# A six-layer cross network on one core: turning the first group on TensorE, and reordering the last two groups

## The chip, the cores and the metric

The kernel runs on one core of one Trainium2 chip. The metric is the device time of one execution in microseconds (us). A profiled execution also gives its span, from the first to the last instruction. In the profiled execution of the kernel before, the time is 1.8 us more than the span (491.88 against 490.1). Positions inside an execution are counted from the start of the span.

Names: TensorE is PE in the profile, VectorE is DVE, ScalarE is ACT, GpSimd is POOL, SyncE is SP. "SPq" and "ACTq" lines are DMA issues by SyncE and ScalarE. PE "products" are matmuls of a layer; "turning" is a transposition on PE by a product with the identity. A "filler" is a product whose result nobody reads; it only keeps PE busy. The "granted clock" is the share of its full clock that PE was given according to the profile's records: 1.00 is full, 0.50 is half.

## The reference

```python
# x0: [16384, 416], ws: [6, 416, 416], bs: [6, 416], all bf16
x = x0
for l in range(6):
    proj = einsum('bd,de->be', x, ws[l]) + bs[l]
    x = x0 * proj + x
return x
```

## The kernel before

The 16384 rows are 8 groups of 2048 rows, each of 4 chunks of 512. The 416 features are three tiles of 128 and a tail of 32. A job (g, l) is layer l of group g; 48 jobs run in an order that interleaves the groups. Rows are kept transposed (features on the partitions), so a job is three tiles of 12 full products (128 x 128 weights, 512 columns), 4 products for the tail rows of the weights (`rows32`), and, batched over some jobs (`tails`), the 32 output features of the tail. ScalarE adds the bias and takes the result out of PSUM, VectorE multiplies with x0 and adds x.

The head: of group 0, chunks 0 and 1 are loaded as they lie in memory ("natural") and turned on PE; chunks 2 and 3 come by DMA transposes.

```python
    add("act", lambda h: h.dma_start(bs_sb[0:L, :], bs[:, :]), ...)
    load_nat(0, 0, 2)          # chunk 0, its first half: 208 KB
    load_nat(0, 2, KK)         # and its second
    load_wm(0, "sp")           # the weights of layer 0: 312 KB
    load_nat(1, 0, KK)         # chunk 1: 416 KB
    load_w3(0, "sp")
    make_wbd(0)
    half = slice(2 * CH, GC)
    ...                        # transpose of the tail
    for t in range(NT):
        add("sp", lambda h, t=t: h.dma_start_transpose(
            x0s[0][:, t * GC + 2 * CH:(t + 1) * GC], g0[half, t * P:(t + 1) * P]), ...)
    ...
def first_job():
    transposed_chunk(0)        # 12 + 4 turns on PE, 2 ScalarE and 2 VectorE copies out of PSUM
    ...                        # bias turned
    full(g, l, 0, ba, True, True, chunks=[0])
    transposed_chunk(1)
    ...
    full(g, l, 0, ba, True, True, chunks=[1])
    full(g, l, 1, bb, True, True, chunks=[0, 1])
    full(g, l, 0, ba, True, True, chunks=[2, 3])
    rows32(g, l, 0, ba, False)
    ...
```

The end: group 6 leaves by DMA transposes out of the transposed form (4 small ones for the tail, 3 large ones, "main turns"), then one store of 1664 KB. Layer 5 of group 7 is computed with the rows on the partitions: its input is turned on PE (`to_rows`) and four row sets kk (every fourth row) are computed and stored one by one. (The first line of the cut stands below `output` in the kernel.)

```python
    where[((LAST, L - 2), 0)] = batches[-1]     # the last tails: behind tile 0 of job (7, 4)
    ...
    def output(g):
        ...
        for j in range(NJ):
            add("sp", lambda h, ...: h.dma_start_transpose(ost[...], x3s[s3][q, :]), ...)  # tail
        if g == LAST - 1:
            turn(0)
            turn(1)
        turn(2)
        ...                                      # the store, 1664 KB
    ...
    to_rows(0, bka)
    layer_rows(0, bkb)
    to_rows(1, bka)
    layer_rows(1, bkb)
    layer_rows(2, bka)
    layer_rows(3, bkb)
```

The job order ends (6,4), (7,4), (6,5), and then (7,5) in the row form.

Of the kernel before, what the change touches and what calls it, by code (L numbers as in the profile page):

```python
# [198 lines left out]
def bass_standalone__cross_network_dcn__recsys_kernel(  # L199
# [57 lines left out]
    def x0_tok(s, t, j):  # L257
        return ("x0", s, t, j)
# [21 lines left out]
    def load_wm(l, eng):  # L280
        add(eng, lambda h: h.dma_start(wm[l][:, :, :], ws[l, 0:NT * P, :].rearrange("(t p) f -> p t f", p=P)),
            writes=[("wm", l)], lane=f"wm{l}", batch=0)
# [189 lines left out]
    def load_nat(j, k0, k1):  # L472
        add("sp", lambda h: h.dma_start(x0n[:, j, k0:k1, :], perm(g0, j)[:, k0:k1, :]),  # L473
            writes=[("nat", j, k) for k in range(k0, k1)], lane=f"nat{j}{k0}", batch=0)

    add("dve", lambda h: h.memset(warm[:, :], 0.0), writes=["warm"])
    add("act", lambda h: h.activation(warm[:, :], warm[:, :], ACT_F.Identity, bias=0.0, scale=1.0),
        reads=["warm"], writes=["warm"])
    add("act", lambda h: h.dma_start(bs_sb[0:L, :], bs[:, :]), writes=["bs_sb"], lane="bs", batch=0)
    load_nat(0, 0, 2)  # L480
    load_nat(0, 2, KK)
    load_wm(0, "sp")
    load_nat(1, 0, KK)
    load_w3(0, "sp")
    make_wbd(0)
    half = slice(2 * CH, GC)
    add("sp", lambda h: h.dma_start_transpose(tw[NTW - 1][:, half], g0[half, D - P:D]),  # L487
        writes=[("tw", NTW - 1, j) for j in (2, 3)], lane="Tb0", batch=0)
    for t in range(NT):
        add("sp", lambda h, t=t: h.dma_start_transpose(  # L490
            x0s[0][:, t * GC + 2 * CH:(t + 1) * GC], g0[half, t * P:(t + 1) * P]),
            writes=[x0_tok(0, t, j) for j in (2, 3)], lane=f"x0_00{t}", batch=0)
    load_wm(1, "sp")
    load_w3(1, "sp")
    load_group(1)
# [2 lines left out]
    make_wbd(1)  # L498
    make_wbd(2)

    for _ in range(14):
        add("pe", lambda h: h.matmul(psum[:, 7 * CH:7 * CH + P], ident[:, :], ident[:, :], start=True, stop=True),
            reads=["ident"], writes=[("ps", 7)])

    def psum_t(b):
        return psum[:, b * CH:(b + 1) * CH].bitcast(BF16)
# [30 lines left out]
    def first_job():  # L537

        g, l = 0, 0
        start_job(g, l)  # L540
        transposed_chunk(0)
        bt = 7
        for t in range(NT):
            add("pe", lambda h, t=t: h.transpose(
                psum_t(bt)[:, t * 8:t * 8 + L], bs_sb[0:L, t * P:(t + 1) * P], ident[0:L, 0:L]),
                reads=["bs_sb", "ident"], writes=[("ps", bt)])
        for j in range(NJ):
            q = slice(j * T32, (j + 1) * T32)
            add("pe", lambda h, j=j, q=q: h.matmul(
                psum_t(bt)[q, NT * 8:NT * 8 + L], bs_sb[0:L, NT * P:D], ident[0:L, 0:L],  # L550
                is_transpose=True, tile_position=(0, j * T32)),
                reads=["bs_sb", "ident"], writes=[("ps", bt)])
        add("act", lambda h: h.activation(
            bias[:, :, :], psum_t(bt)[:, 0:32].rearrange("p (t l) -> p t l", l=8)[:, :, 0:L], ACT_F.Copy),
            reads=[("ps", bt)], writes=["bias"])
        ba, bb = [4, 5, 6, 7], [0, 1, 2, 3]
        full(g, l, 0, ba, True, True, chunks=[0])
        transposed_chunk(1)
        for j in (2, 3):
            q = slice(j * T32, (j + 1) * T32)  # L560
            add("act", lambda h, q=q, j=j: h.dma_start(
                x0s[0][q, XW:XW + CH], tw[NTW - 1][P - T32:P, j * CH:(j + 1) * CH]),
                reads=[("tw", NTW - 1, j)], writes=[("x03q", 0, j)], lane="x03_00", batch=0)
        full(g, l, 0, ba, True, True, chunks=[1])
        full(g, l, 1, bb, True, True, chunks=[0, 1])
        full(g, l, 0, ba, True, True, chunks=[2, 3])
        rows32(g, l, 0, ba, False)
        evacuate(g, l, 0, ba, [0, 1], 2, vector=[2, 3])
        full(g, l, 1, bb, True, True, chunks=[2, 3])
        rows32(g, l, 1, bb, False)  # L570
        rows32(g, l, 2, ba, True)
        evacuate(g, l, 1, bb, list(range(NJ)), 2)
        full(g, l, 2, ba, False, True, lambda j: evacuate(g, l, 2, ba, [j], 1))
        finish_tile(g, l, NT)
        tails([(g, l)])
# [19 lines left out]
    def output(g):  # L595

        s, s3 = xset[(g, L)], xtail[(g, L)]
        def turn(t):
            add("sp", lambda h: h.dma_start_transpose(
                ost[:, :, t * P:(t + 1) * P], xs[s][:, t * GC:(t + 1) * GC]),  # L600
                reads=[("x", s, t, j) for j in range(NJ)], writes=[("ost", t)], lane="ot", batch=g)

        if g < LAST - 1:
# [3 lines that stand above are left out]
            q = slice(j * T32, (j + 1) * T32)  # L607
            add("sp", lambda h, j=j, q=q: h.dma_start_transpose(
                ost[:, j * KK:(j + 1) * KK, NT * P:D], x3s[s3][q, :]),
                reads=[("x3", s3)], writes=[("ost", NT, j)], lane="ot", batch=g)  # L610
# [4 lines that stand above are left out]
        rows = out[g * GC:(g + 1) * GC, :]  # L615
        o = ost[:, :, :].rearrange("p (j k) f -> p j k f", j=NJ)
        parts = [("(j k p) f -> p j k f", 0, NJ)]
        if g == 0:
            parts = [("(j p k) f -> p j k f", 0, 2), ("(j k p) f -> p j k f", 2, NJ)]
        for pat, j0, j1 in parts:  # L620
            add("sp", lambda h, pat=pat, j0=j0, j1=j1: h.dma_start(
                rows[j0 * CH:j1 * CH, :].rearrange(pat, j=j1 - j0, k=KK), o[:, j0:j1, :, :]),
                reads=[("ost", t) for t in range(NT)] + [("ost", NT, j) for j in range(NJ)],
                writes=[("out", g, j0)], lane="out", batch=g)
        free_x.append(s)
        free_3.append(s3)

    items = []
    where = {(b[min(1, len(b) - 1)], 0): b for b in batches[:-1]}
    where[((LAST, L - 2), 0)] = batches[-1]  # L630
    del where[((0, 0), 0)]
    for jb in order[1:-1]:
        for i in range(NT):
            items.append(("tile", jb, i))
            if (jb, i) in where:
                items.append(("tails", where[(jb, i)]))


    single = 0
# [84 lines left out]

    first_use = {"x5": True, "on": True}

    def to_rows(kp, bks):

        for j in range(NJ):
            for h2 in range(2):  # L730
                for t in range(NT):
                    o = h2 * CH + t * P
                    add("pe", lambda h, j=j, t=t, kk=2 * kp + h2, o=o: h.transpose(  # L733
                        psum_t(bks[j])[:, o:o + P], xcol(t, j, kk), ident[:, :]),
                        reads=[stok(t, j), "ident"], writes=[("ps", bks[j])])
        for h2 in range(2):
            for j in range(NJ):
                q = slice(j * T32, (j + 1) * T32)
                o = h2 * CH + NT * P
                add("pe", lambda h, j=j, q=q, kk=2 * kp + h2, o=o: h.matmul(  # L740
                    psum_t(bks[j])[:, o:o + T32], x3col(j, kk), ident[q, q], is_transpose=True,
                    tile_position=(j * T32, 0)),
                    reads=tok3 + ["ident"], writes=[("ps", bks[j])])
        for j in range(NJ):
            extra = x0_all(s5) + x03_toks(s5) if first_use.pop("x5", None) else []
            eng = "act" if j % 2 == 0 else "dve"
# [46 lines left out]
        add("dve", lambda h: h.tensor_tensor(o, o, x5v, ALU.add),  # L793
            reads=[("on", j, kk), ("x5n", j, kk // 2)], writes=[("on", j, kk)])

    def nat_store(kk, j0, j1, lane, eng="sp"):
        dst = out[LAST * GC:B, :].rearrange("(j p k) f -> p j k f", j=NJ, k=KK)[:, j0:j1, kk, :]
        add(eng, lambda h: h.dma_start(dst, on[:, j0:j1, kk, :]),
            reads=[("on", j, kk) for j in range(j0, j1)], writes=[("out7", kk, j0)], lane=lane, batch=0)

    bka, bkb = take(NJ), take(NJ)
    last = KK - 1

    def layer_rows(kk, bks):
        nat_rows(kk, bks, True)
        for j in range(NJ):
            nat_full(kk, j, bks[j], False)
            nat_mul(kk, j, bks[j])
            if j:
                nat_add(kk, j - 1)  # L810
            if kk == last and j == 2:
                nat_store(kk, 0, 2, "out7_3")
            if kk == last and j == 3:
                nat_store(kk, 2, 3, "out7_4")
        nat_add(kk, NJ - 1)
        if kk < last:
            nat_store(kk, 0, NJ, f"out7_{kk}")
        else:
            nat_store(kk, NJ - 1, NJ, "out7_5", "act")

    to_rows(0, bka)
    layer_rows(0, bkb)
    to_rows(1, bka)
    layer_rows(1, bkb)
    layer_rows(2, bka)
    layer_rows(3, bkb)

    pr.emit()

# [27 lines left out]
```

## Time and profile before

| What | Value |
|---|---|
| median of the first 3 runs | 490.07 us (489.60 to 490.86) |
| the execution that was profiled | 491.88 us, span 490.1 us |
| PE busy | 97% of the span |
| first `rows32` of layer 1 starts | 26.63 us |
| last full product starts | 469.17 us |
| store of group 6 issued | 477.58 us |
| last store issued | 485.09 us |

The page gives, for each engine, busy time, share and instructions; below, the chain of work that ended last, by engine.

```profile
span 490.1 us, 8003 instructions
...
PE 476.6 (97%) x3205; PEld 199.7 (41%) x3205; DVE 403.7 (82%) x709; ACT 340.6 (69%) x368; POOL 11.5 (2%) x37
...
PE 93%; DVE 2%; SPq 2%; DMA 1%; ACT 1%; issue 0%; DVEq 0%
```

The timeline of PE in the head (start, length, engine, line, operation, operands, count, and in brackets the idle time before it with what ended it) shows the two waits for the transposed chunks. L418 is the full products, L430 is `rows32`, L518 is the turning:

```profile
6.76 0.81 PE L418 MATMUL ps<-x,wm 128*128 128x512 bf16 x3 [1.19 <-DMA wm<-in_ws_dram]
7.71 0.84 PE L518 MATMUL ps<-ident,x 128*128 128x128 bf16 x12
...
12.15 0.39 PE L418 MATMUL ps<-x,wm 128*128 128x512 bf16 x1 [0.53 <-DMA x<-in_x_dram]
14.16 1.04 PE L418 MATMUL ps<-x,wm 128*128 128x512 bf16 x4 [1.62 <-DMA x<-in_x_dram]
15.13 0.46 PE L430 MATMUL ps<-x,w 32*128 32x512 bf16 x4
...
26.63 0.61 PE L430 MATMUL ps<-x,w 32*128 32x512 bf16 x8 [0.41 <-DVE x L408]
```

The windows view (stretch; its length; busy time, with the number of instructions, of PE, its weight loads, VectorE, ScalarE and GpSimd, in this order; then granted PE clock, DMA share, GB/s) shows the clock reduced after these waits:

```profile
16.00:17.00 1.00, 1.00 (x4) 0.38 (x3) 1.00 (x3) 0.73 (x1) 0.39 (x2) 0.50 1.30 272
17.00:18.00 1.00, 1.00 (x3) 0.15 (x1) 1.00 (x4) 0.00 (x0) 0.82 (x4) 0.50 0.75 156
18.00:19.00 1.00, 1.00 (x10) 0.16 (x10) 0.35 (x1) 0.16 (x1) 0.07 (x1) 0.63 1.27 247
```

And the end, in the same view and in the DMA issues of the timeline (L608 is group 6's tail transposes, L599 its main turns, L621 its store, L798 group 7's stores):

```profile
480.00:484.00 4.00, 3.23 (x23) 1.53 (x21) 3.75 (x14) 2.60 (x6) 0.00 (x0) 1.00 1.07 341
484.00:488.00 4.00, 0.00 (x0) 0.00 (x0) 1.06 (x3) 0.00 (x0) 0.00 (x0) 0.80 1.11 332
```

```profile
458.53 6.23 SPq L608 DMA_TRANSPOSE ost<-x  x4
467.73 6.51 SPq L599 DMA_TRANSPOSE ost<-x  x3
477.58 0.37 SPq L621 DMA_DIRECT2D out_dram<-ost  x1
478.00 7.75 SPq L798 DMA_DIRECT2D out_dram<-x  x5
```

In the end the DMA engines are full (share over 1, 332 to 341 GB/s) for longer than PE works, although the chain names PE.

### The profile page before, as it was taken

Reading aid. Unit: us, or ns where it says so; the run is one execution under the profiler, and the core shown is the slowest. Engines: PE = TensorE matmul, PEld = TensorE weight load, DVE = VectorE, ACT = ScalarE, POOL = GpSimd, SP = SyncE. Lnnn points to the kernel's source line nnn. Section 1 sums busy time; section 2 is a strip of 40 time slices with the busy share of each in tenths; the row PEclk is TensorE's granted clock in tenths of the full one; section 3 lists DMA queues with packets and bytes.
Section 4 is the critical chain, followed back from the end, with each engine's and each line's share of the span. In section 5 each row is a group of like instructions: output and inputs, shape, how many; then the busy total and the mean of one; then the engine's idle time right before and its main releaser. Section 6 shows DMA issues by size and latency. Waiting matters only on the chain.

```text
span 490.1 us, 8003 instructions
## 1 busy us (share of the span) xinstructions
PE 476.6 (97%) x3205; PEld 199.7 (41%) x3205; DVE 403.7 (82%) x709; ACT 340.6 (69%) x368; POOL 11.5 (2%) x37
## 2 busy tenths in 40 slices
PE   6899999999999999999999999999999999999994
PEld 4233434444444444444444444444444444444462
DVE  1578888888888888888888888888888888888895
ACT  3466677677677677767767767767767767767783
POOL 1110400000000000000000000000000000000000
PEclk9899999999999999999999999999999999999998
DMA  8965977000000468258506962580000136043468
GB/s 185 200 146 133 167 134 140 1 0 1 2 0 18 76 181 180 53 98 228 94 3 127 229 106 27 114 279 1 2 1 0 34 63 185 1 86 84 123 130 278
DMA packets 132521, 47.91 MB, mean 98 GB/s; under 512 B 111930, under 2 KB 131588, under 8 KB 132484
## 3 DMA queue, kind: packets, MB, share of 16 engines
q1 hardware_dynamic: 132232, 47.23, 43.8%
q8 instruction: 25, 0.41, 0.4%
q10 hardware_dynamic: 252, 0.18, 0.1%
q14 instruction: 12, 0.10, 0.1%
HBM read 5.12 MB, written 13.63 MB: 38 GB/s over the span
## 4 chain that ended last, share of the span: by engine, by line
PE 93%; DVE 2%; SPq 2%; DMA 1%; ACT 1%; issue 0%; DVEq 0%
PE ps L418 74%; PE ps L430 8%; PE ps L443 6%; PE ps L448 2%; PE ps L758 2%; DMA x<-in_x_dram 1%; DVE x L391 1%; DVE tw L386 1%; SPq L490 1%; PE ps L733 1%; ACT tw L377 0%; SPq L286 0%; SPq L473 0%; SPq L487 0%; ACT x L786 0%
## 5 line engine op out<-in xcount | busy, mean ns | idle before, releaser
L377 ACT ACTIVATE tw<-ps,bias 128x1024 bf16<-128x1024 f32 (+1 forms) x295 | 299.5, 1070 | 134.4 <-PE ps L430 107.2
L418 PE MATMUL ps<-x,wm 128*128 128x512 bf16 x1692 | 381.5, 380 | 3.9 <-DMA x<-in_x_dram 2.1
L418 PEld LDWEIGHTS ps<-x,wm 128*128 128x128 bf16 x1692 | 159.0, 98 | 219.9 <-issue 30.1
L386 DVE TENSOR_TENSOR tw<-tw,x 128x1024 bf16<-128x1024 bf16 (+1 forms) x285 | 193.0, 683 | 66.9 <-ACT tw L377 66.6
L391 DVE TENSOR_TENSOR x<-tw,x 128x1024 bf16<-128x1024 bf16 (+1 forms) x285 | 181.4, 677 | 0.0
L430 PE MATMUL ps<-x,w 32*128 32x512 bf16 x564 | 44.8, 382 | 0.8 <-DVE x L408 0.8
L443 PE MATMUL ps<-x,wm 128*32 128x512 bf16 x564 | 38.7, 380 | 0.0
L404 ACT ACTIVATE ts<-ps,bias 128x512 bf16<-128x512 f32 x47 | 28.7, 700 | 0.0
L430 PEld LDWEIGHTS ps<-x,w 32*128 32x128 bf16 x564 | 9.1, 92 | 34.4 <-issue 33.0
L443 PEld LDWEIGHTS ps<-x,wm 128*32 128x32 bf16 x564 | 13.8, 96 | 15.7 <-issue 2.9
L408 DVE TENSOR_TENSOR x<-ts,x 128x512 bf16<-128x512 bf16 x47 | 18.6, 419 | 0.0
L406 DVE TENSOR_TENSOR ts<-ts,x 128x512 bf16<-128x512 bf16 x47 | 18.6, 418 | 0.0
L448 PE MATMUL ps<-x,wbd 128*32 128x512 bf16 x188 | 18.3, 379 | 0.0
L293 POOL COPY wbd<-w 32x32 bf16<-32x32 bf16 x24 | 9.4, 392 | 44.2 <-DMA w<-in_ws_dram 43.1
L758 PE MATMUL ps<-wm,x 128*128 128x416 bf16 x48 | 9.2, 341 | 0.0
L786 ACT ACTIVATE x<-ps 128x416 bf16<-128x416 f32 x15 | 7.1, 532 | 1.2 <-PE ps L758 1.1
L448 PEld LDWEIGHTS ps<-x,wbd 128*32 128x32 bf16 x188 | 5.0, 97 | 5.1
L531 DVE COPY x<-ps 128x512 bf16<-128x512 bf16 x2 | 0.8, 425 | 7.3 <-PE ps L523 7.3
L758 PEld LDWEIGHTS ps<-wm,x 128*128 128x128 bf16 x48 | 5.1, 115 | 3.9 <-issue 1.4
L361 DVE SCALAR_TENSOR_TENSOR tw<-ps,bias,x 128x512 bf16<-128x512 f32 x2 | 1.4, 746 | 5.9 <-PE ps L430 5.9
L788 DVE TENSOR_TENSOR x<-x,x 128x416 bf16<-128x416 bf16 x15 | 5.5, 371 | 0.4
L528 ACT ACTIVATE x<-ps 128x512 bf16<-128x512 bf16 x4 | 2.2, 594 | 5.0 <-PE ps L518 5.0
(36 smaller groups left out, 37.1 us busy)
## 6 DMA issues: line engine op xcount, KB each, us to landing
out_dram<-ost SPq DMA_DIRECT2D x6, 1664.0 KB, 7.0
x<-in_x_dram SPq DMA_DIRECT2D x5, 416.0 KB, 7.2
wm<-in_ws_dram SPq DMA_DIRECT2D x6, 312.0 KB, 3.2
out_dram<-ost SPq DMA_DIRECT2D x2, 832.0 KB, 5.1
out_dram<-x SPq DMA_DIRECT2D x3, 416.0 KB, 6.9
x<-Tb SPq DMA_DIRECT2D x28, 32.0 KB, 1.8
ost<-x SPq DMA_TRANSPOSE x49, 3.6
w<-in_ws_dram SPq DMA_DIRECT2D x24, 26.0 KB, 2.4
```

The lines of the kernel that those rows point to most:

```text
L293: add("pool", lambda h, q=q: h.tensor_copy(wbd[l][q, q], w3[l][q, NT * P:D]), reads=[("w3", l, j)], writes=[("wbd", l)])
L377: add("act", lambda h, a=a, w=w, b0=b0: h.activation(tw[r][:, a * CH:(a + w) * CH], psum[:, b0 * CH:(b0 + w) * CH], ACT_F.Identity, bias=b ...
L386: add("dve", lambda h, a=a, e=e: h.tensor_tensor(tw[r][:, a * CH:e * CH], tw[r][:, a * CH:e * CH], x0s[s0][:, i * GC + a * CH:i * GC + e * ...
L391: add("dve", lambda h, a=a, e=e: h.tensor_tensor(xs[so][:, i * GC + a * CH:i * GC + e * CH], tw[r][:, a * CH:e * CH], src(i, a, e), ALU.ad ...
L404: add("act", lambda h: h.activation(ts[r][:, :], bank(b), ACT_F.Identity, bias=bias[:, 3, l:l + 1], scale=1.0), reads=[("ps", b), "bias"], ...
L406: add("dve", lambda h: h.tensor_tensor(ts[r][:, :], ts[r][:, :], x0s[s0][:, XW:XW + CH], ALU.mult), reads=[("ts", r)] + x03_toks(s0), writ ...
L408: add("dve", lambda h: h.tensor_tensor(x3s[so][:, :], ts[r][:, :], src, ALU.add), reads=[("ts", r)] + stok, writes=[("x3", so)], hold=True)
L418: add("pe", lambda h, t=t, j=j: h.matmul(bank(banks[j]), wm[l][:, t, ecols], src(t, j, j + 1), start=(first and t == 0), stop=(not first a ...
L430: add("pe", lambda h, q=q, j=j: h.matmul(bank(banks[j]), w3[l][q, ecols], src[q, :], start=first, stop=not first, tile_position=(j * T32, 0)),
L443: add("pe", lambda h, t=t, j=j, src=src, l=l, b=b: h.matmul(bank(b, j * T32, (j + 1) * T32), wm[l][:, t, NT * P:D], src(t, j, j + 1), star ...
L448: add("pe", lambda h, j=j, s3=s3, l=l, b=b: h.matmul(bank(b, j * T32, (j + 1) * T32), wbd[l][:, j * T32:(j + 1) * T32], s3, start=False, s ...
L758: add("pe", lambda h, t=t: h.matmul(bank(b, n=D), xcol(t, j, kk), wm[l][:, t, :], start=(first and t == 0), stop=(not first and t == NT - 1)),
```

## The change

Its intent: no DMA transposes in front of group 0, with chunks turned on PE between the first products; and, in the end, group 6 finished earlier by moving one tile of group 7's layer 4 behind it, with the turning of that tile held back ("rows turned in parts"). The diff cut to its core:

```diff
+    load_wm(0, "act")
+    add("act", lambda h: h.dma_start(bs_sb[0:L, :], bs[:, :]), ...)
     load_nat(0, 0, 2)
     load_nat(0, 2, KK)
-    load_wm(0, "sp")
-    load_nat(1, 0, KK)
+    for j in range(1, NJ):
+        load_nat(j, 0, KK)
     load_w3(0, "sp")
-    ... dma_start_transpose of the tail and of the 3 tiles of chunks 2 and 3
 ...
+        keep_busy(8, 3)                      # 8 filler products with the identity
         full(g, l, 0, ba, True, True, chunks=[0])
         transposed_chunk(1)
+        transposed_chunk(2)
         full(g, l, 0, ba, True, True, chunks=[1])
+        transposed_chunk(3)
         full(g, l, 1, bb, True, True, chunks=[0, 1])
 ...
-    where[((LAST, L - 2), 0)] = batches[-1]
+    where[((LAST - 1, L - 1), 0)] = batches[-1]     # the last tails: behind tile 0 of (6, 5)
 ...
+    late = items.index(("tile", (LAST, L - 2), NT - 1))
+    items.append(items.pop(late))                   # tile 2 of (7, 4) behind all of (6, 5)
 ...
-    to_rows(0, bka)
-    layer_rows(0, bkb)
-    to_rows(1, bka)
-    layer_rows(1, bkb)
+    turn_main(0, bka, (0, 1))
+    turn_tails(0, bka)
+    nat_rows(0, bkb, True)
+    turn_main(0, bka, (2,))                         # needs the late tile
+    rows_out(0, bka)
+    layer_full(0, bkb)
+    turn_main(1, bka, (0, 1, 2))
+    ...
+    nat_store(0, 2, 0, NJ)                          # two row sets in one store, 832 KB
```

## The prediction

> **What bounds it now.** From 27 to 483 us the kernel is bound by TensorE (PE): the page gives PE 97% busy and the waits view lists only 6 us of PE waits, all in the head. Two stretches differ.
>
> *Head.* The timeline shows PE's first tile of layer 0 ending only at 15.5 us, because half of group 0 arrives by DMA transposes (256-byte packets in the trace, about 230 GB/s): PE waits until 12.15 and again until 14.15 us. The idle PE is then granted half its clock (windows: 0.50 to 0.67 from 15 to 19 us), which agrees with "TensorE: Matmul & The Clock Gate", section "The HAM clock gate", of the Trainium skill. So tile 1 ends at 18.9; VectorE idles 1.6 us for it, then works without gap until 26.6, when PE gets the tail of the next layer.
>
> *End.* The chain of waits names PE, but the windows view shows the DMA engines saturated (share 1.04 to 1.12, 330 to 353 GB/s) from 479 to 488.7 us. They drain the stores of groups 6 (issued at 477.6) and 7, 1664 KB each: 3.3 MB at 340 GB/s = 9.8 us. The last store, issued at 485.1, waits behind these. The end is set by when group 6's store starts, not by PE (last matmul 483.2).
>
> **Head after.** Loads of four natural chunks and the weights: 1976 KB in packets of 832 to 3328 bytes, at 300 to 380 GB/s from 2 us: estimate, all landed by 8 us. PE turns chunks in about 0.9 us each (timeline: 0.84 + 0.40 us, overlapping), ScalarE copies two per chunk (1.1 us). My schedule: first product 6.4, chunk 1's at 9.0, tile 0 complete at 13.4 (was 15.5), full clock, tile 1 complete at 15.2 (was 18.9). VectorE saves its 1.6 us, and the next layer's tail is ready at 22.9 instead of 26.6. Gain 3.5 us (2.5 to 4.5), all on the critical path.
>
> **End after.** The tails of (7,4) and (6,5) move two tiles later (+5.8 us). Group 6's four tail transposes stand first in the DMA queue before its three main turns, and take 6.2 us to issue (458.5 to 464.8 now, then 3 us of slack until tile 0 is ready at 467.7). Moved to 464.4, they end at 470.6, so the turns start 2.9 us later; they keep the DMA engines busy for 7.8 us (469.0 to 476.8 now). Group 6's store then starts 2.9 us later relative to PE. The drain of 3.3 MB follows; 1664-byte packets for 1.2 MB of it save about 0.4 us. Net loss 2.3 us.
> Also, layer 4's tile 2 of group 7 now comes last; turning it waits about 1.5 us for VectorE (its backlog now ends at 472.9, PE's last product 469.4). PE ends about 1.1 us later, hidden behind the drain.
>
> **Sum.** 490.1 - 3.5 + 2.3 = 488.9 us; range 486.2 to 490.6. Faster by over 2%: 1%; within 2%: 98%; slower: 1%.
>
> **What would show it.** Right: PE clock 1.0 at 15 us, rows of layer 1 at about 23 us; group 6's store 2.9 us later relative to the last layer-4 product; DMA share above 1 to the end. Wrong: an idle DMA before the end, or that store earlier.
>
> **What would make it wrong.** Slower natural loads, or clock lost between chunks (head gain 1 to 2 us); tail transposes or turns issued faster (the end gains: 486); a longer wait of PE on VectorE.

## The result, and the profile after

| | before | after |
|---|---|---|
| median | 490.01 us (4 runs) | 492.34 us (4 runs, 492.18 to 492.50) |
| profiled execution: span | 490.1 us | 490.6 us |

The ratio of the times is 1.0045, 95% interval 1.0028 to 1.0063. All ratios and intervals here are those of fast runs of the same rounds; they are not quite the ratios of the medians. The change made the kernel slower by 0.45%; 488.9 us was predicted, and the range ended at 490.6.

The page after, then the same timeline of the head (L516 is now the turning), and the end in both views (L604 tail transposes, L595 main turns, L617 group 6's store, L803 group 7's):

```profile
span 490.6 us, 8035 instructions
...
PE 474.3 (97%) x3191; PEld 203.2 (41%) x3245; DVE 405.8 (83%) x713; ACT 343.4 (70%) x372; POOL 11.9 (2%) x37
...
PE 90%; DVE 4%; ACT 2%; issue 2%; DMA 1%; SPq 0%; DVEq 0%
```

```profile
4.84 0.82 PE L516 MATMUL ps<-ident,x 128*128 128x128 bf16 x6 [0.60 <-DMA x<-in_x_dram]
...
7.25 1.49 PE L418 MATMUL ps<-x,wm 128*128 128x512 bf16 x3
8.53 1.49 PE L516 MATMUL ps<-ident,x 128*128 128x128 bf16 x12
...
15.83 0.40 PE L430 MATMUL ps<-x,w 32*128 32x512 bf16 x4
...
25.77 0.61 PE L430 MATMUL ps<-x,w 32*128 32x512 bf16 x8 [0.41 <-DVE x L408]
```

```profile
470.00:475.00 5.00, 4.15 (x38) 2.63 (x34) 4.37 (x13) 3.76 (x6) 0.00 (x0) 1.00 1.13 209
475.00:476.00 1.00, 1.00 (x27) 0.86 (x28) 1.00 (x4) 0.03 (x1) 0.00 (x0) 1.00 2.30 117
476.00:477.00 1.00, 1.00 (x12) 0.48 (x5) 1.00 (x3) 0.98 (x2) 0.00 (x0) 1.00 0.33 56
480.00:484.00 4.00, 4.00 (x28) 2.02 (x26) 3.75 (x14) 3.33 (x7) 0.00 (x0) 1.00 1.06 348
484.00:489.00 5.00, 0.03 (x1) 0.00 (x0) 1.86 (x6) 0.05 (x1) 0.00 (x0) 0.89 1.08 368
```

```profile
463.50 5.00 SPq L604 DMA_TRANSPOSE ost<-x  x4
468.54 7.92 SPq L595 DMA_TRANSPOSE ost<-x  x3
478.72 0.37 SPq L617 DMA_DIRECT2D out_dram<-ost  x1
480.61 5.91 SPq L803 DMA_DIRECT2D out_dram<-x  x4
```

What is to be seen: no PE wait for DMA transposes any more, and yet the first `rows32` of layer 1 comes at 25.77, only 0.86 us earlier than in the profile of before. The first three products take 1.49 us where they took 0.81, and the 12 turns of chunk 1 take 1.49 where they took 0.84. In the end, group 6's tail transposes start 5.0 us later and its store 1.1 us later, although PE's last full product is 0.85 us earlier.

**How every trace was cut.** All 14 profiles have the same middle: from the start of the first `rows32` of layer 1 to the start of the last full product there are 442.54 or 442.55 us in each. So a span is a head (up to that `rows32`), 442.5 us, and an end (from the last full product on). The table of all runs is read that way; its times are in us, and differences of rounded times can be off by 0.01. "Clock full" is the first full clock in the clock records.

| Run | clock full at | head | group 6's store after the last full product | last store issued, same count | end | span | median (runs) |
|---|---|---|---|---|---|---|---|
| before | 5.1, half from 15.3 to 18.7 | 26.63 | 8.41 | 15.92 | 20.91 | 490.1 | 490.01 (4) |
| e0, before again | 10.2 | 24.52 | 8.41 | 15.92 | 20.91 | 488.0 | 491.37 (6) |
| after | 10.0 | 25.77 | 10.40 | 17.57 | 22.30 | 490.6 | 492.34 (4) |
| e11, after again | 10.4 | 25.94 | 11.17 | 17.57 | 23.04 | 491.5 | 493.46 (6) |
| e1, head only | 10.6 | 26.04 | 8.79 | 15.92 | 21.26 | 489.8 | 490.86 (5) |
| e2, end only | 10.7, half from 471.5 to 474.9 | 24.56 | 10.38 | 19.25 | 23.05 | 490.2 | 491.04 (6) |
| e3, tails early | 11.4 | 26.48 | 5.31 | 17.57 | 20.12 | 489.1 | 490.24 (5) |
| e4, half store | 9.8 | 24.71 | 8.36 | 15.92 | 18.17 | 485.4 | 487.40 (4) |
| e5, gap filled | 4.9 | 23.79 | 11.38 | 17.56 | 23.23 | 489.6 | 491.39 (5) |
| e6, no filler | 10.9 | 25.69 | 10.56 | 17.56 | 22.45 | 490.7 | 492.03 (5) |
| e7, weights behind | 7.8 | 24.34 | 11.00 | 17.57 | 22.87 | 489.8 | 491.57 (5) |
| e8, put together | 5.0 | 23.95 | 6.98 | 17.04 | 19.58 | 486.1 | 487.87 (5) |
| e9, its end with before's head | 11.3 | 25.22 | 5.32 | 17.04 | 19.59 | 487.4 | 489.14 (5) |
| e10, e8 without the split | 6.3 | 25.62 | 5.29 | 17.57 | 20.12 | 488.3 | 489.75 (6) |

The medians of the kernel before that ran beside the experiments are 489.94 (e0 to e3), 490.17 (e4 to e7), 489.76 (e8 to e10) and 490.36 (e11).

### The profile page after: what moved, and what is told of

Read it like the earlier page. It is cut to its first block, busy times and chain, and to the rows that moved or that the text cites. A ratio compares the mean times of both kernels' runs of the same rounds, so it can differ in the third digit from the quotient of the medians.

```text
span 490.6 us, 8035 instructions
## 1 busy us (share of the span) xinstructions
PE 474.3 (97%) x3191; PEld 203.2 (41%) x3245; DVE 405.8 (83%) x713; ACT 343.4 (70%) x372; POOL 11.9 (2%) x37
## 4 chain that ended last, share of the span: by engine, by line
PE 90%; DVE 4%; ACT 2%; issue 2%; DMA 1%; SPq 0%; DVEq 0%
PE ps L418 72%; PE ps L430 8%; PE ps L443 5%; ACT tw L377 2%; DVE x L391 2%; PE ps L448 2%; DVE tw L386 1%; PE ps L761 1%; DMA x<-in_x_dram 1%; PE ps L516 1%; PE ps L731 0%; PE ps L521 0%; ACT ts L404 0%; ACT x L789 0%; DVE ts L406 0%
## 5 line engine op out<-in xcount | busy, mean ns | idle before, releaser
L418 PE MATMUL ps<-x,wm 128*128 128x512 bf16 x1638 | 373.6, 380 | 5.6 <-issue 3.3
L526 ACT ACTIVATE x<-ps 128x512 bf16<-128x512 bf16 x8 | 4.3, 594 | 5.9 <-PE ps L516 5.9
L791 DVE TENSOR_TENSOR x<-x,x 128x416 bf16<-128x416 bf16 x15 | 5.5, 371 | 1.9 <-ACT x L789 1.7
L796 DVE TENSOR_TENSOR x<-x,x 128x416 bf16<-128x416 bf16 x16 | 5.6, 367 | 0.0
```

The costliest lines, as they stand in the source:

```text
L418: add("pe", lambda h, t=t, j=j: h.matmul(bank(banks[j]), wm[l][:, t, ecols], src(t, j, j + 1), start=(first and t == 0), stop=(not first a ...
```

## The experiments

Two theories stood against each other for each part. For the head: "half clock" (PE gets its full clock late and the changed head is made of PE work, so that it pays for it) against "too much PE work" (the extra turns and fillers simply cost more than the waits they replace). For the end: "drain" (the DMA engines' queue sets the end) against "chain" (PE and VectorE set it, as the profile's chain says).

### e0: the kernel before, once more

No edit.

> The kernel before, once more, as a control. The profile of before came from an execution of 491.9 us, slower than every timed one (489.6 to 490.9), and it holds a stretch of 3.4 us at half clock (15.3 to 18.7 us). Theory 'clock luck': that stretch is in some executions only; spans then spread over some 2 us and the shorter ones show no half clock after 10 us. Rival 'profile overhead': every listed execution shows a span near 490.1 and the half clock at the same place.

Measured: 491.37 us median of 6 (489.77 to 491.95), ratio to itself 1.0027, interval 1.0014 to 1.0039. The profiled execution took 489.77 us, and there is no half clock between 10.2 and 484.6 us in it. Its head:

```profile
6.36 1.44 PE L418 MATMUL ps<-x,wm 128*128 128x512 bf16 x3 [0.79 <-DMA wm<-in_ws_dram]
7.59 1.49 PE L518 MATMUL ps<-ident,x 128*128 128x128 bf16 x12
...
13.60 1.04 PE L418 MATMUL ps<-x,wm 128*128 128x512 bf16 x4 [1.22 <-DMA x<-in_x_dram]
14.57 0.39 PE L430 MATMUL ps<-x,w 32*128 32x512 bf16 x4
...
24.52 0.61 PE L430 MATMUL ps<-x,w 32*128 32x512 bf16 x8 [0.41 <-DVE x L408]
```

"Clock luck" holds. The profile of before, from which I predicted, is of a slow execution: its 490.1 us span and 491.88 us time lie above every timed run of the first batch, and its head is 26.63 us where four other traces with this head (e0, e2, e4, e9) show 24.52, 24.56, 24.71 and 25.22. From the first `rows32` to that of layer 1 it needs 11.5 us, e0 9.94 us, as do all twelve other traces; the 1.6 us idle of VectorE that I meant to win back is not there in e0.

It also warns about small effects: the same code under another name differs by 0.27% with an interval that excludes 1. The times of e0 lie in two clusters, near 490 and near 491.6. The timed runs have no trace, but the record lists the mean granted clock of each. It does so for 50 executions of this kernel: the profiled one of before, the six of e0, and 43 that ran beside the experiments. The eight with a clock of 0.993 or less took 491.33 to 492.21 us, the 42 with 0.994 or more took 489.38 to 491.03. One stretch of 3.41 us at half clock lowers the mean over 490 us by 0.0035 (an estimate from before's records), so one such stretch fits the step between the clusters; where it lay in the timed runs is not shown. Four of e0's six met it and three of the 43 beside; why stays open.

### e1 and e2: one part alone

e1 applies the diff's hunks up to `first_job`, with the pattern of group 0's store; e2 applies all the others.

> Only the change's head (group 0 turned wholly on TensorE, weights on the other queue, 8 filler products), the end as before. The after trace has the first tail of layer 1 ready 0.9 us earlier than the before trace, where 3.5 was predicted, and the clock full only at 10.0 us instead of 5.1. Theory: the head alone moves the time by -1 to +0.5 us against before (489 to 490.5). Rival (head is worth the predicted 3.5 us and the end eats 6): 486.5 us.

> Only the change's end, the head as before. Theory 'drain': group 6's store is issued 2 to 3 us later, the DMA engines are saturated up to the end, time +2 us (492). Rival 'chain' (TensorE and VectorE set the end, TensorE's last matmul 1.1 us later, last store then): +1 us (491), with a DMA that is not saturated before the last store.

Measured: e1 490.86 us, ratio 1.0018 (1.0006 to 1.0030); e2 491.04 us, ratio 1.0024 (1.0011 to 1.0038). So each part alone is slower, by 0.9 and 1.1 us of the medians; together 2.0, where the whole change measured 2.3. Both ratios are smaller than the 0.27% by which the same code differed in e0, so these sizes are uncertain; the sign rests on the traces too (heads of 25.8 to 26.5 us in after, e11, e1 and e3, against 24.5 to 25.2; ends of 22.3 to 23.2 in all six traces with the whole changed end, against 20.91). e1's head is 26.04 us, above 24.5 to 25.2 of the good executions of the old head. Its time is above the range I had put down (489 to 490.5) and far from the rival's 486.5. In e2, group 6's store starts 10.38 us after the last full product, 2.0 later than before, as "drain" asked. Its DMA share stays at 1.05 to 1.10 from 480 to 488 us, against "chain", but its time is the 491 that "chain" had asked. So e2 cannot judge drain against chain: its last store is issued later than in any other run (19.25), because PE got half clock from 471.5 to 474.9 us, just after it had waited for VectorE, and its 12 products of layer 5 took 3.88 us there instead of 2.27.

### e3: the tails early

```diff
-    where[((LAST - 1, L - 1), 0)] = batches[-1]
+    where[((LAST, L - 2), 0)] = batches[-1]
```

> The changed kernel with one line back: the last batch of tails stands behind tile 0 of group 7's layer 4, as before, so that group 6's tail transposes are issued 5.8 us earlier and its tiles are ready 2.9 us earlier. Theory 'drain': group 6's store is issued about 474 to 475 us instead of 478.7, the drain no longer sets the end, time 2 us shorter than after (490.3), the last store now waits for VectorE alone. Rival 'chain': no change (492.3).

Measured: 490.24 us, ratio to before 1.0005 (0.9993 to 1.0017); 2.1 us below the 492.34 of after (of other rounds). The store of group 6 is issued 5.31 us after the last full product instead of 10.40, and the end shrinks from 22.30 to 20.12. The DMA engines now run empty before the last stores:

```profile
476.00:480.00 4.00, 4.00 (x48) 2.20 (x46) 3.03 (x9) 3.26 (x6) 0.00 (x0) 1.00 1.07 340
480.00:482.00 2.00, 2.00 (x16) 1.11 (x18) 2.00 (x8) 1.51 (x3) 0.00 (x0) 1.00 0.20 58
...
484.00:486.00 2.00, 0.73 (x5) 0.23 (x2) 1.85 (x7) 0.75 (x2) 0.00 (x0) 1.00 0.52 182
```

With the queue out of the way, the last store needs 2.55 us from issue to the end of the span, where it needed 4.99 in before and 4.74 in after. "Drain" holds for after, and here "chain" has taken over: the last store is issued at 17.57, as in after.

### e4: half of group 6 not stored

```diff
+        if g == LAST - 1:
+            parts = [("(j k p) f -> p j k f", 0, 2)]
```

> The kernel before with half of group 6's rows not stored (832 KB less; wrong on purpose). In its profile the end (from the last 128-row product of layer 5 to the end of the span) takes 20.9 us. Theory 'drain': the DMA engines are saturated there at 340 GB/s, so the end shrinks by about 2.4 us to 18.5, where the chain of VectorE and the last store takes over. Rival 'chain' (as the profile's chain of waits names it): the end stays within 0.3 us of 20.9.

The result is wrong on purpose: 832 KB are not written. Measured: 487.40 us, ratio 0.9944 (0.9931 to 0.9958). The end takes 18.17 us instead of 20.91, 2.7 less; 2.4 was expected. The last store is issued at 15.92, exactly as in before, so nothing on PE, ScalarE or VectorE moved. In the kernel before, too, the drain set the end; the page's chain (PE 93%) does not show it.

```profile
477.00:481.00 4.00, 4.00 (x30) 2.22 (x27) 3.75 (x14) 3.29 (x7) 0.00 (x0) 1.00 1.06 343
...
483.00:486.00 3.00, 0.00 (x0) 0.00 (x0) 0.13 (x1) 0.00 (x0) 0.00 (x0) 0.71 0.42 141
```

### e5: fillers in the gap

```diff
-        for t, k in seq + [(NT, k) for k in range(KK)]:
+        for n, (t, k) in enumerate(seq + [(NT, k) for k in range(KK)]):
+            if j == 0 and n == 2 * NT:
+                keep_busy(8, 7)
```

> The changed kernel with 8 more filler products between the two halves of chunk 0's turning, where TensorE idles 0.6 us at 4.2 us. Theory 'half clock': the head is slow because TensorE runs at half clock up to 10.0 to 11.4 us, and an earlier full clock shortens it; expected full clock by 6.6 to 8.6 us and the first tail of layer 1 at 24 to 25 us instead of 25.8 to 26.5, time 1 to 1.5 us shorter than after. Rival 'too much TensorE work': the head stays at 25.8 or grows by the fillers' 0.3 us.

Measured: full clock at 4.9 us, earlier than the 6.6 to 8.6 expected; head 23.79 us: 2.0 us shorter than after, with 8 products more to do. "Too much PE work" falls.

```profile
6.46 0.81 PE L418 MATMUL ps<-x,wm 128*128 128x512 bf16 x3
7.11 0.83 PE L518 MATMUL ps<-ident,x 128*128 128x128 bf16 x12
...
13.85 0.39 PE L430 MATMUL ps<-x,w 32*128 32x512 bf16 x4
...
23.79 0.61 PE L430 MATMUL ps<-x,w 32*128 32x512 bf16 x8 [0.41 <-DVE x L408]
```

The time, 491.39 us, is only 0.95 below after's, because this trace's end is 0.9 us longer: group 6's store starts 11.38 us after the last full product instead of 10.40. In the windows of after, the stretch 475 to 477 us shows the large transposes stalling (117 and 56 GB/s between 209 and more). The packet records show 16 KB instruction fetches at that moment in all six traces (after, e1, e5, e6, e7, e11) where the transposes' rate falls from about 215 GB/s to under 20 in single half microseconds, for 1 to 2.5 us in all, after which it rises to 290. In e0 and e2 the fetch came at the end of the transposes or behind it, and there is no such dip. That the fetch causes it was not tested: it is a coincidence seen six times.

### e6: without the fillers of the change

```diff
-        keep_busy(8, 3)
```

> The changed kernel without its 8 filler products before the first product. If the fillers only delay (they end at 7.25 us, the inputs of the first product are there at 6.7): head 0.5 us shorter. If they keep the clock up: full clock one window (3.4 us) later, head up to 1.5 us longer.

Measured: 492.03 us, head 25.69 (after 25.77). The first product starts at 6.43 instead of 7.25, and the clock is full at 10.9 instead of 10.0. That is within the 10.0 to 11.4 of the four traces that have these fillers (after, e11, e1, e3), so an effect of the fillers on the clock is not shown. The fillers are not what costs.

### e7: the first weights behind chunk 0

```diff
-    load_wm(0, "act")
 ...
     load_nat(0, 2, KK)
+    load_wm(0, "sp")
```

> The changed kernel with the first weights back on the SP queue behind chunk 0. Chunk 0's second half then lands by 3.9 us instead of 4.8 (as before), TensorE has no gap at 4.2 us; the weights land at about 5 us, before the first product needs them. Theory 'half clock' and 'queue shared' both: head 0.5 to 2 us shorter than 25.8; no change if the start does not matter.

Measured: 491.57 us; head 24.34 us, full clock at 7.8. PE has no gap at 4.2 us. In after, the second half of chunk 0 let PE start at 4.84; here all 12 turns run from 3.37 without a wait. The second half of chunk 0 lands at 4.01 us, in after at 4.79, while the weights land at 6.20 instead of 4.29: on the other queue they had taken bandwidth from the chunk that PE waited for. This agrees with the Trainium skill, "DMA: Bandwidth & Descriptors", section "Issuing engines are not separate DMA queues": DMAs of different issuing engines share the same 16 DMA engines and interleave. As in e5, a longer end (22.87) hides part of the gain in the time.

### e8, e9, e10: a version that beats both

e8 takes from the change its head and its end, with e7's order of loads, e3's early tails, fillers that start earlier on the tile of ones, and 8 products of layer 5 ahead of the turning that waits for VectorE. e9 is the same end on the head of before. e10 is e8 without the 8 products moved.

```diff
-            add("pe", ... h.matmul(bank(b, n=P), ident[:, :], ident[:, :], ...), reads=["ident"], ...)
+            add("pe", ... h.matmul(bank(b, n=P), ones[:, :], ones[:, :], ...), reads=["ones"], ...)
-    keep_busy(14, 7)
+    keep_busy(22, 7)
 ...
     nat_rows(0, bkb, True)
+    for j in range(NJ):
+        nat_full(0, j, bkb[j], False, (0, 1))       # e8 and e9: weight tiles 0 and 1
     turn_main(0, bka, (2,))
     rows_out(0, bka)
-    layer_full(0, bkb)
+    layer_full(0, bkb, (2,))
```

> Everything learnt, put together: the changed head with the first weights behind chunk 0 and 22 fillers that start 0.85 us earlier (on the tile of ones, ready before the identity); the tails early as in e3; and 8 of layer 5's products per row (of weight tiles 0 and 1) placed before the turning that waits for VectorE. Theory: full clock by 4.5 to 7.8 us, head 23.5 to 24.3 us (before 24.5); TensorE no longer waits 1.65 us in the end, end 18.6 us (before 20.9, e3 20.1); span 485.0 to 485.5, time about 487 (before 490). If the wait only moves, the end stays at 20.1 and the time at 488.5.

> The same end as e8 with the head of the kernel before. Theory: end 18.6 us, head 24.5 (26.6 with an unlucky stretch of half clock), time about 487.7 and more spread than e8. Tells what the changed head is worth when its clock is full: 0.3 to 1 us here.

> e8 without moving the 8 products ahead of the turning: the end of e3. Theory: end 20.1 us, 1.5 us longer than e8; rival 'drain sets it still': the same as e8.

Measured: e8 487.87 us, ratio 0.9962 (0.9950 to 0.9973): faster than before by 0.38%, and 4.5 us below the median of after (of other rounds). e9 489.14 us, 0.9990 (0.9978 to 1.0002). e10 489.75 us, 0.9987 (0.9973 to 1.0000). Every run of e8 (487.57 to 488.92) lies below every run of before. e9 missed what was expected (end 18.6 us, time 487.7), as e8's end did.

e8 against e9 is the head alone: the ends are 19.58 and 19.59, the heads 23.95 and 25.22, and the medians differ by the same 1.27 us. So the idea of the changed head is worth something once its clock is full early. How much is less sure than that figure: e9's head is itself the slowest of the four usual ones, and against e0's 24.52 e8's head gains 0.6 us. The ends agree although e8's store of group 6 starts 1.7 us later than e9's (6.98 against 5.32; an instruction fetch at 471.4 us fell on the last of its transposes): in e8, e9 and e10 the last store needs 2.5 us from issue to the end of the span, as in e3, so the drain no longer sets the end.

e8 against e10 tells the worth of the split: the end is 0.54 us shorter (19.58 against 20.12), where 1.5 was expected. Most of the wait moved: in e8's chain of waits ScalarE stands between the turning and the next products, copying out the turned rows and then the results, and PE waits for it:

```profile
470.01 0.13 PE ps L731 x2
...
470.16 1.62 ACT x L753 x2
471.78 1.65 ACT x L789 x4
...
473.47 0.35 PE ps L772
```

e10's head should have been e8's and was not (25.62 us with the clock full at 6.3): PE waited 1.7 us for chunk 1's load in that execution, and 0.3 us in e8's. Its times fall in two clusters (near 488.4 and near 489.9). What slows that load in some executions was not tested.

### e11: the changed kernel, once more

No edit.

> The changed kernel once more, as a control of its own spread, since the kernel before gave 489.9 and 491.4 us under two names. Theory: head 25.5 to 26.5 us with the clock full at 10 to 11.4 us, fixed middle of 442.5 us, end 22.0 to 23.1 us, time 491.5 to 493, 1.5 to 2.5 above before. If it comes out below 490.5, the difference between the two kernels is the luck of the clock alone.

Measured: 493.46 us (491.95 to 493.77), ratio 1.0056 (1.0035 to 1.0076); head 25.94, clock full at 10.4, end 23.04. The loss is there again, and the luck of the clock alone doesn't make it: all ten executions of the changed kernel (491.95 to 493.77, mean clock 0.996 or 0.997) lie above the 42 of before that had a clock of 0.994 or more. The median lies above the 491.5 to 493 that I had put down.

## Why the prediction was wrong

The sum was 490.1 - 3.5 + 2.3. The term that failed is the first one, "Gain 3.5 us (2.5 to 4.5), all on the critical path". By e1 the head costs about 0.9 us instead. The end term had the right sign and mechanism and was somewhat too large.

**The head, step one: the base was an unlucky execution.** I read "was 15.5", "was 18.9" and "26.6" from a profile whose execution was 1.9 us slower than the median. A stretch of half clock from 15.33 to 18.74 us, which I had seen, I took for a property of the kernel. It is a property of that execution: in e0 the head is 24.52 us, and by the mean clocks listed under e0 such a stretch was in 8 of 50 executions. About 2.1 of the 3.5 us were nobody's to win. The page's own evidence was there to be read: the profiled execution's 491.88 us against 490.07 in the times, and my sum set out from 490.1 as a time, where the span of a usual execution is about 488.

**The head, step two: "full clock".** My schedule assumed it for the changed head from the first product on. The clock was full at 10.0 us (10.4 in e11, 10.6 in e1, 11.4 in e3), after PE had idled 0.6 us at 4.2 us. The three first products took 1.49 us and chunk 1's turning 1.49 us. In the five traces with that idle time (after, e11, e1, e3, e6) the clock is full at 10.0 to 11.4 us, in the four without it (e5, e7, e8, e10) at 4.9 to 7.8. With the clock full at 4.9 us (e5) the head is 23.79 us, with 7.8 (e7) 24.34, so the late clock costs 1.4 to 2.0 us. It hurts the changed head more than the old one because the old one waits for transposes up to 13.6 us anyway (e0), while the new one is PE work from end to end. The prediction had named a lost clock as a risk, but with a gain of 1 to 2 us left; against e0, after's head is 1.25 us longer. The old head runs at half clock as long (10.2 us in e0), but behind a wait that it has anyway.

**The head, step three: a schedule that was too tight.** Even with full clock (e5) I was off by 0.9 us: first product 6.46 (predicted 6.4), chunk 1's product 9.40 (9.0), `rows32` of tile 0 starting at 13.85 (complete at 13.4), layer 1's `rows32` 23.79 (22.9). Turning each of the three later chunks holds PE for 1.1 to 1.2 us in e5 (7.11 to 8.30, 8.30 to 9.40, 10.06 to 11.15), where 0.9 was assumed; by this estimate that is 0.7 of the 0.9. Steps two and three are the 2.9 us between the predicted 22.9 and the measured 25.77; step one is the 2.1 us between the base I took and a usual one.

**The end: right.** Predicted: tail transposes 5.8 us later, the store 2.9 us later relative to the last full product, net loss 2.3 us. Measured: the tail transposes start at -4.82 us relative to the last full product instead of -10.64, so 5.8 later; the store 2.0 later (2.8 in e11); the end 1.4 us longer (2.1 in e11), and e2's time 1.1 us above before. The four tail transposes were issued in 5.0 us, not 6.2; that is the term that was a little too large. The reason is shown by e3 and e4: moving one line back takes 2.2 us off the end, and taking 832 KB out of the store takes 2.7 off the end of before with all engines' work unmoved. The drain itself was shorter in after: its written packets span 9.8 us instead of 10.4, with packets of 1664 bytes among them, against a predicted gain of 0.4.

**The wait for VectorE, predicted 1.5 us, hidden behind the drain: right.** The last store is issued 17.57 us after the last full product instead of 15.92, 1.65 later (1.1 predicted). In e3, where the drain no longer hides it, it sets the end. One thing was not foreseen: such a wait can cost the clock once more (e2, half clock from 471.5 us).

**What the intent missed.** "Group 6 ends earlier" was true of its last tile, and yet its store started later, because the four tail transposes stand first in the same DMA queue and their data was moved two tiles back. A queue served in order starts with its first entry's data, however early the others' is.

## What to carry to other kernels

Before predicting from a profile, compare the profiled execution's own time with the timed runs, and take a wait or a clock dip seen once for luck until a second trace shows it. When DMA waits are exchanged for PE work at the start of a kernel, ask at which clock that work will run, and keep PE busy without a gap from its first instruction. At the end of a kernel, count the bytes still to be written and divide by the rate: if that exceeds the remaining work, only the start of the first large store counts, and what stands before it in its queue.

## What the Trainium skill lacked or had wrong

- "TensorE: Matmul & The Clock Gate", section "Part 1: The HAM clock gate (the "warmup" mystery)", says the window is 3.4 us and free-running and that the warm-up therefore varies from run to run. The traces agree: the half-clock stretches inside before and e2 last 3.41 us, and the first full clock came between 4.9 and 11.4 us. The page advises not to model this, as under 1% of a span. True here (2.1 of 490 us), but a tuned kernel's changes are of that size, and the page, which says that the warm-up varies, lacks the warning that a half-clock stretch inside the kernel can be in the one profiled execution and not in most others (8 of 50 executions of before, by their mean clock).
- The same page lacks how busy a window must be. Dividing the time before the first full clock into stretches of 3.41 us counted back from it, PE's matmuls were busy 90 to 100% of the stretch that ended in full clock, and at most 89% of every earlier one, in all 14 traces. Turns count here as busy: they fill the second half of before's stretch from 1.68 to 5.09 us. In after a gap of 0.6 us (82% busy) was enough to miss a window. This is worked out from the records, not a documented rule.
- The same page puts the return to half clock down to a whole idle window of about 3.4 us. Here it came without one: the longest idle time of PE in the stretch before it was 1.6 us (before) and 0.4 us (e2). The loss did not follow one share of busy time either: a stretch with 46% busy lost it (before, at 15.3 us), 75% lost it (e2, at 471.5 us), and 50% (e10) and 65% (e0) kept it. What decides it stays open.
- "TensorE: Matmul & The Clock Gate" warns that clock records can be unreliable. A case that it lacks: the clock row and column of the profile show 1.00 before their first record. In after they show full clock from 0 to 10 us, while 12 turns took 1.49 us, against 0.84 later in the same trace.
- "Perfetto Trace Analysis", section "Per-instruction lifecycle: what the profiler-reported window actually captures", says that a DMA's data movement lies outside its profiled window. It fits that the chain of waits ends with VectorE, before the last store's issue; the number: 4.99 us from the last store's issue to the end in before and 2.55 us with an empty queue (e3).
- "Runtime: NRT & Kernel Launch", section "Instruction fetch mechanics", lacks what a fetch does to DMA transposes under way, and no other page has it: a fetch of 16 KB coincided with 1 to 2.5 us of slowed transposes in six traces; the store behind them started at 10.4 to 11.4 us after the last full product where the tails were late (after, e5, e6, e7, e11), and at 10.4 in e2, which had no dip. The cause was not tested.
